# Three cell visits moved to the borders between the feed-forward's products, and the gate products of later chunks moved in front of a mix, into a feed-forward bank

## The chip, the cores and the metric

The kernel runs on one core of a Trainium2 chip. The metric is device time in microseconds (us). TensorE does the matrix products, VectorE and GpSimd the elementwise work, ScalarE the activations, SyncE issues the DMAs (transfers between HBM and on-chip memory). Each engine works through its own queue in order and waits on semaphores of the others. Products land in PSUM, eight banks of 128 partitions by 512 floats; a bank can be written anew once its last reader is through.

## The reference

Two blocks follow each other: an mLSTM cell over 4 batches, 8 heads, 768 steps and head size 40, and a feed-forward block with leaky ReLU, 320 to 2048 to 320, over all 3072 tokens.

```python
for t in range(S):
    m_new = np.maximum(f_gate[:, :, t] + m, i_gate[:, :, t])
    f_stab = np.exp(f_gate[:, :, t] + m - m_new)
    i_stab = np.exp(i_gate[:, :, t] - m_new)
    m = m_new
    C = f_stab[:, :, None, None] * C + i_stab[:, :, None, None] * np.einsum('bhd,bhe->bhde', vt, kt)
    n = f_stab[:, :, None] * n + i_stab[:, :, None] * kt
    h_tilde = np.einsum('bhde,bhe->bhd', C, qt)
    nq = np.einsum('bhd,bhd->bh', n, qt)[:, :, None]
    denom = np.maximum(np.abs(nq), 1.0)
    o = 1.0 / (1.0 + np.exp(-o_gate[:, :, t]))
    y[:, :, t] = o * h_tilde / denom
...
h = x @ w_in
g = np.maximum(0.01 * h, h)
return (g @ w_out).astype(np.float32)
```

## The kernel before

**Chunks and groups.** The 768 steps are cut into six chunks of 128. A *step* `s` of the program is one chunk of one batch, `s = 4c + b`, 24 in all. The recurrence within a chunk is done with matrix products over two halves of 64 steps, and a state is carried from half to half and chunk to chunk. The feed-forward block of chunk `g` (512 tokens, called a group) runs on TensorE while the cells of later chunks are worked out. The cells are cut into pieces and put between the feed-forward's matmuls by hand.

**Feed-forward units.** An ordinary group has 30 units. The *first product* has 8 pairs, each in two units (`pair` in `ff_units`): a pair owns two banks `ph`, its first unit takes 12 matmuls (L909, weights of 64 rows by 128 columns), its second 8, and then two leaky ReLUs on ScalarE (L917) write the activations `acts` and so free the banks. The *second product* (`fast_units`) is a Strassen-like scheme with seven products for each of two token blocks, 14 units of 16 recorded matmuls each (L984, 128 by 128 weights, bank `po`), in the order p1, p2, p6, p7, p4, p5, p3. p1's result is copied by ScalarE (L1003) and `acts` blocks are summed in place by VectorE (L1002 after p1(0) and p1(1), L1007 after p1(1)); p2 is added by VectorE (L1011), which frees its bank; p6, p7 and p4 are copied by ScalarE and added by GpSimd; p5 and p3 are added by VectorE (L1036, L1041). p6 needs the sums of L1007, p7 reads `s3_at` by the weight mix `t3`.

Units are numbered through: group 1 has units 0 to 29 (first product 0 to 15, second 16 to 29), group 2 has 30 to 59 (30 to 45, 46 to 59), group 3 has 60 to 89. Groups 4 and 5 (`three_units`) compute their first product in three parts and have no cells between. The work planned for a unit stands directly behind the unit's matmuls in every queue.

**Cells between the units.** From chunk 2 on, two steps are done at a time. `ready(s)` (READY) transposes keys and queries on VectorE (L537), multiplies queries by decays (L543), and lets GpSimd carry the state on (L630), place the values (L391), scale the keys to `vu` (L510) and mask the decays (L482), whose exponentials ScalarE takes in small portions (L490) in front of later units. A *visit* (VISITS, `u_parts`) issues what remains of the exponentials, and then the score products and state sums on TensorE (`sd`, L652 and L657, 64-row and 64-column weights). VectorE multiplies the scores by the decays (L662, into `qn`) and adds to the state (L634). After the visit stands `feed`, the DMAs of the step four later. A *mix* (MIXES, `u_mix`) multiplies `qn` by state and values on TensorE (`pT`, L745, 128-row and 64-column weights), then VectorE transposes (L752), takes denominators, gates (L756), and GpSimd scales (L759), VectorE transposes back (L763), and the result goes out to `x_dr`, from which `gather_x` reads `xT` for the next group.

**Gate products.** `gates` and `gates_exp` work out a chunk's cumulative gates; `gates_T` (L341) transposes them on TensorE into a tile `tg` (L344, L349, 32-row weights), which VectorE copies out to `gT` and `gL` (L354, L356). `state_next` and the exponentials of the following chunk need these. Units UG say where this is done for chunks 3, 4 and 5.

**Banks.** There are two pools of four PSUM banks: `psf` (tag `mm`) for the feed-forward's `ph` and `po`, `psc` (tag `c`) for the cells' tiles `sd`, `pT` and `tg`. Within a pool a new tile takes a bank whose last tile has been released, and TensorE waits for the engine that reads that tile last.

The plan of the middle stage is this (L1207 on):

```python
VISITS = (5, 14, 27, 35, 46, 58, 67, 76)
MIXES = (7, 17, 29, 37, 51, 60, 69, 77)
READY = ((7, 8), (18, 25), (32, 33), (41, 42), (51, 54), (62, 66), (69, 72))
GATES = ((1, 4), (20, 25), (38, 44))
UG = (18, 37, 62)
PER = NF + 14
```

Of the kernel before, what the change touches and what calls it, by code (L numbers as in the profile page):

```python
# [10 lines left out]
F32 = mybir.dt.float32  # L11
# [11 lines left out]
def kernel(  # L23
# [28 lines left out]
    P = 128  # L52
    BH = B * H
    NB = S // P
# [24 lines left out]
    psf = ctx.enter_context(tc.tile_pool(name="psf", bufs=4, space=PSUM))  # L79
    psc = ctx.enter_context(tc.tile_pool(name="psc", bufs=4, space=PSUM))  # L80
# [257 lines left out]
            nc.tensor.matmul(t[:], lhsT=ident[:], rhs=ident[:], start=True, stop=True)  # L338

    def gates_T(c, bu):  # L340
        tg = psc.tile([P, 5, BH], F32, name="tg", tag="c")  # L341
        kinds = 3 if c == 1 else 2
        for n in range(kinds):
            nc.tensor.transpose(tg[:, n, :], bu[:, n, :], ident[:BH, :BH])  # L344
        gT[c] = wk.tile([P, 3, BH], F32, name="gT")
        if c > 0:
            for u in range(2):
                last = SL * (u + 1) - 1
                nc.tensor.matmul(  # L349
                    tg[:, 3 + u, :], lhsT=bu[:, 2, last : last + 1].to_broadcast([BH, P]), rhs=ident[:BH, :BH],  # L350
                    start=True, stop=True,
                )
            gL[c] = f0[:, ts(c % 2, 2 * BH)].rearrange("p (u n) -> p u n", u=2)
        nc.vector.tensor_copy(gT[c][:, :kinds], tg[:, :kinds, :])  # L354
        if c > 0:
            nc.vector.tensor_copy(gL[c], tg[:, 3:, :])  # L356
# [424 lines left out]
    def open_parts():  # L781

        cells_stack.close()
        kp = ctx.enter_context(tc.tile_pool(name="kp", bufs=1))
        for key in ("raw", "low", "dif"):
            parts["w", key] = [kp.tile([P, WC], F32R, name=f"w_{key}{n}") for n in range(QN)]
        for key in ("low", "dif"):
            parts["x", key] = kp.tile([P, B, KC * P], F32R, name=f"x_{key}")
        parts["tmp"] = [kp.tile([P, KC * P], F32, name=f"tmp{n}") for n in range(2)]
        parts["n"] = 0  # L790
# [255 lines left out]
    def u_gates(c):  # L1046
        gates_T(c, bus.pop(c)[0])
# [78 lines left out]
    def first_chunk():  # L1126

        ffs, narrow = [], {}

        def ff(j, b0, b1):  # L1130
            if not ffs:
                ffs.extend(ff_units(0))
            ffs[0](j, b0, b1)

        def step(n, e=None):
            if (n, e) not in narrow:
                narrow[n, e] = narrow_weights(n, e)
            next(narrow[n, e], None)

        acts_of = {  # L1140
            "ld": load, "lo": load_o, "lw": load_weights, "g": gates, "ge": gates_exp, "warm": warm,
            "ug": lambda c: gates_T(c, bus[c][0] if c == 0 else bus.pop(c)[0]),
            "tr": u_transpose, "tc": transpose_copy, "ab": lambda n: spread_first(bus[0][1], n), "abw": spread_mask,
            "exp": lambda n: run(prep_exp(n)), "vu": prep_vu, "tiles": prepare_tiles, "sc": u_scores, "scm": scores_mix,
            "st": state, "stc": state_copy, "val": u_values, "den": values_den, "o": prep_o, "gate": gate,
            "gp": gate_scale, "nw": step, "ps": prepare_step, "x": u_x, "xc": x_copy, "ff": ff,
            "warmer": warmer, "idle": idle, "fd": feed, "ll": load_late,
        }
        for line in ORDER.split("\n"):
            for what in line.split(";"):  # L1150
                name, *args = what.split() or [None]
                if name:
                    acts_of[name](*map(int, args))
        return ffs[1]

    E = mybir.EngineType
    with tc.manual_schedule(engines={E.PE, E.DVE, E.Activation, E.Pool}):
# [46 lines left out]
                    if s + NL < NS:  # L1204
                        feed(s + NL)

        VISITS = (5, 14, 27, 35, 46, 58, 67, 76)  # L1207
        MIXES = (7, 17, 29, 37, 51, 60, 69, 77)
        READY = ((7, 8), (18, 25), (32, 33), (41, 42), (51, 54), (62, 66), (69, 72))
        GATES = ((1, 4), (20, 25), (38, 44))  # L1210
        UG = (18, 37, 62)
        PER = NF + 14
        SPLIT = (82, 83, 84, 85, 86, 87, 90, 91, 93, 96, 99, 102)
        plan = collections.defaultdict(list)
# [1 line left out]
        def at_unit(unit, fn, *args):  # L1216
            plan[unit].append((fn, args))

        def visit_steps(p):
            return (2 * B + 2 * p, 2 * B + 2 * p + 1) if p < len(VISITS) else ()  # L1220

        def gather():

            while at["past"] and mixed_steps and mixed_steps[0] // B == at["group"] + 1:
                gather_x(mixed_steps.pop(0))
# [22 lines left out]
        mixed_steps = []  # L1248
        for p, unit in enumerate(VISITS):
            c = 2 + p // 2  # L1250
            if p % 2 == 0 and c + 1 < NB:
                at_unit(GATES[p // 2][0], gates, c + 1)
                at_unit(GATES[p // 2][1], gates_exp, c + 1)
            for s in visit_steps(p):
                at_unit(unit, u_parts, s)
            for s in visit_steps(p + 2):
                at_unit(unit, feed, s)
            for s in visit_steps(p):
                at_unit(MIXES[p], mix, s)
            for s in visit_steps(p + 1):  # L1260
                at_unit(MIXES[p], load_late, s, 2)
            if p % 2 == 1 and c + 1 < NB:
                at_unit(UG[p // 2], u_gates, c + 1)
            for n, s in enumerate(visit_steps(p + 1)):
                at_unit(READY[p][n], ready, s)

# [14 lines left out]
        for g in range(1, NB):  # L1281
# [3 lines left out]
            for i in range(len(ffs)):  # L1285
# [8 lines left out]
                gather()  # L1294
                if unit == MIXES[-1]:
                    open_parts()
# [38 lines left out]
```

## Time and profile before

| what | us |
|---|---|
| median of 3 runs | 486.96 |
| lowest and highest | 486.33, 487.30 |
| the profiled execution, its own time | 486.61 |
| its span in the profile | 484.5 |
| TensorE busy | 478.6 |
| VectorE busy | 364.6 |
| ScalarE busy | 196.1 |
| GpSimd busy | 159.4 |

The span is from the first to the last recorded instruction; the 2.1 us between it and the execution's own time lie around it. The granted TensorE clock is full throughout (1.0). Rows of the chain of waits give the start of a piece and its length, both in us, the engine, the tile and the line; `x20` is the number of instructions merged. Rows of a timeline give start, length, engine, line, operation, the tiles written and read with their shapes, and in brackets how long the engine had been idle before and what ended that. PE is TensorE, DVE is VectorE, ACT is ScalarE, POOL is GpSimd, SPq the queue of DMAs that SyncE issues.

### The profile page before, as it was taken

What the parts mean: (1) busy time and instruction counts of PE and PEld (TensorE: products, weight loads), DVE (VectorE), ACT (ScalarE), POOL (GpSimd) and SP (SyncE); (2) the same over time, 40 slices, a digit from 0 to 9 for tenths busy, and PEclk for the clock granted to TensorE, in tenths of its full rate; (3) what the DMA queues carried; (4) which work ended last, traced back from release to release, by engine and by line L of the source; (5) the groups of instructions that cost most, each with busy time, mean ns of one, the idle gap of its engine ahead of it and who ended that gap; (6) DMA issues with size and microseconds to landing.
All of it is one profiled execution on the core that took longest, in us unless ns stands there. A gap on an engine that the chain in (4) does not pass through costs nothing.

```text
span 484.5 us, 12804 instructions
## 1 busy us (share of the span) xinstructions
PE 478.6 (99%) x5113; PEld 371.8 (77%) x5113; DVE 364.6 (75%) x601; ACT 196.1 (40%) x499; POOL 159.4 (33%) x207
## 2 busy tenths in 40 slices
PE   8999999999999999999999999999999999999997
PEld 7998655777645489965569985548998899988996
DVE  4689999889917999777887968689899967335611
ACT  2587864743831331405251121524025642156310
POOL 4128024461601826545451645453210002000020
PEclk9999999999999999999999999999999999999999
DMA  7878778896655677667887867774151030100001
GB/s 144 172 164 195 172 163 169 260 211 146 141 129 111 150 144 212 137 158 194 148 193 171 191 149 177 184 183 123 54 225 40 1 108 1 49 8 0 1 1 54
DMA packets 142698, 63.40 MB, mean 131 GB/s; under 512 B 110832, under 2 KB 130864, under 8 KB 142640
## 3 DMA queue, kind: packets, MB, share of 16 engines
q1 hardware_dynamic: 142256, 62.47, 54.4%
q8 instruction: 40, 0.66, 0.6%
q10 hardware_dynamic: 384, 0.13, 0.1%
q14 instruction: 18, 0.15, 0.1%
HBM read 51.68 MB, written 8.27 MB: 124 GB/s over the span
## 4 chain that ended last, share of the span: by engine, by line
PE 95%; DVE 1%; issue 0%; POOL 0%; POOLq 0%; DVEq 0%
PE po L984 32%; PE ph L909 29%; PE ph L835 8%; PE po L945 7%; PE pe L835 4%; PE pT L745 3%; PE sd L652 3%; PE warm L338 2%; PE pa L675 1%; PE sd L657 1%; PE hN L715 1%; PE tk L566 1%; PE tq L552 1%; PE sc L595 1%; PE tkq L580 0%; PE tg L349 0%
## 5 line engine op out<-in xcount | busy, mean ns | idle before, releaser
L909 PE MATMUL ph<-xT,w_in 64*128 64x512 f32 (+1 forms) x680 | 142.3, 569 | 0.0
L909 PEld LDWEIGHTS ph<-xT,w_in 64*128 64x128 f32 x680 | 64.5, 187 | 66.1 <-issue 63.7
L984 PE MATMUL po<-w_out,acts 128*128 128x160 f32 x640 | 91.0, 301 | 0.0
L984 PEld LDWEIGHTS po<-w_out,acts 128*128 128x128 f32 x640 | 87.5, 190 | 3.4 <-ACT w L490 1.5
L917 ACT ACTIVATE acts<-ph 128x512 f32<-128x512 f32 (+1 forms) x68 | 35.1, 567 | 80.3 <-PE ph L909 80.1
L490 ACT ACTIVATE w<-w,gT 128x64 f32<-128x64 f32 (+1 forms) x192 | 51.8, 348 | 28.1 <-POOL w L482 28.1
L630 POOL TENSOR_TENSOR S<-S,f 40x336 f32<-40x336 f32 x36 | 33.9, 941 | 81.2 <-PE pT L745 47.3
L984 PE MATMUL po<-raw,acts 128*128 128x160 f32 x320 | 45.1, 299 | 0.0
L984 PEld LDWEIGHTS po<-raw,acts 128*128 128x128 f32 x320 | 44.0, 190 | 0.0
L1017 POOL TENSOR_TENSOR y<-y,raw 128x160 f32<-128x160 f32 x10 | 5.5, 556 | 112.2 <-ACT y L1016 112.2
L662 DVE TENSOR_TENSOR qn<-w,sd 64x512 f32<-64x512 f32 x40 | 27.4, 684 | 19.9 <-PE sd L657 11.9
L945 PE MATMUL po<-w_out,acts 128*128 128x320 f32 x128 | 36.6, 437 | 0.0
L482 POOL TENSOR_TENSOR w<-w,i 128x512 f32<-128x512 f32 x20 | 32.4, 1618 | 11.7 <-DMA w<-a_dr 11.7
L857 DVE SCALAR_TENSOR_TENSOR acts<-ph,acts 128x512 f32<-128x512 f32 x32 | 20.6, 685 | 20.6 <-ACT acts L855 20.6
L543 DVE TENSOR_TENSOR qn<-kqT,late 64x512 f32<-64x512 f32 x32 | 33.6, 1049 | 1.0
L945 PEld LDWEIGHTS po<-w_out,acts 128*128 128x128 f32 x128 | 23.6, 190 | 9.1
L759 POOL TENSOR_TENSOR xb<-xb,den 128x320 f32<-128x320 f32 x16 | 11.7, 728 | 48.6 <-DVE xb L756 48.6
L855 ACT ACTIVATE acts<-pe 128x512 f32<-128x512 f32 x32 | 17.4, 595 | 19.0 <-PE pe L835 18.9
L763 DVE STREAM_TRANSPOSE x<-xb 128x512 f32<-128x512 f32 x16 | 17.8, 1109 | 7.8 <-POOL xb L759 7.8
L861 ACT ACTIVATE acts<-acts 128x512 f32<-128x512 f32 x32 | 19.7, 633 | 8.1 <-DVE acts L857 8.1
L984 PE MATMUL po<-raw 128*128 128x160 f32 x160 | 22.7, 300 | 0.0
L652 PEld LDWEIGHTS sd<-kqT 40*64 40x64 f32 x640 | 19.6, 135 | 3.7 <-issue 3.7
(166 smaller groups left out, 786.1 us busy)
## 6 DMA issues: line engine op xcount, KB each, us to landing
w<-a_dr SPq DMA_DIRECT2D x40, 128.0 KB, 3.7
rb<-in_k_dram SPq DMA_DIRECT2D x64, 80.0 KB, 2.8
rb<-in_q_dram SPq DMA_DIRECT2D x64, 80.0 KB, 2.6
rb<-in_o_gate_dram SPq DMA_DIRECT2D x64, 80.0 KB, 2.8
xT<-x_dr SPq DMA_DIRECT2D x32, 160.0 KB, 3.1
late<-a_dr SPq DMA_DIRECT2D x32, 128.0 KB, 3.2
x_dr<-x SPq DMA_DIRECT2D x16, 256.0 KB, 3.0
kn<-in_k_dram SPq DMA_DIRECT2D x24, 160.0 KB, 3.4
```

The costliest lines, as they stand in the source:

```text
L482: nc.gpsimd.tensor_tensor(w, w, cm2.unsqueeze(1).to_broadcast([P, H, SL]), op=ALU.add)
L490: yield nc.scalar.activation(w[:, h, :], w[:, h, :], AF.Exp, bias=gT[c][:, 0, bh : bh + 1], scale=1.0)
L543: nc.vector.tensor_tensor(mixed(s)[rows, 1 - r], d["kqT"][rows, 1].rearrange("p (h t) -> p h t", t=SL), d["ea"][rows], op=ALU.mult,)
L630: nc.gpsimd.tensor_tensor(new, old, g, op=ALU.mult)
L652: nc.tensor.matmul(bank[1 - u][toks, h, :], lhsT=kqT[rows, 0, ts(h, SL)], rhs=kqT[rows, 1, ts(h, SL)], start=True, stop=True,)
L662: nc.vector.tensor_tensor(mixed(s)[toks, u], w[toks], bank[1 - u][toks], op=ALU.mult)
L835: nc.tensor.matmul(ph[r][:], lhsT=parts["w", key][n][part, at : at + P], rhs=xs[key][part, slot, :], start=start and slot == 0, stop=stop ...
L857: nc.vector.scalar_tensor_tensor(fs[r], in0=ph[r][:], scalar=1.0 + EPS, in1=fs[r], op0=ALU.mult, op1=ALU.add,)
L909: nc.tensor.matmul(ph[r][:, cols], lhsT=w_row(r, slot, j), rhs=xT[DP * r : DP * (r + 1), slot, bs, :], start=(slot == 0), stop=(slot == KC ...
L917: nc.scalar.activation(acts[:, f, cols], ph[r][:, cols], AF.Prelu, alpha=0.01)
L945: nc.tensor.matmul(po[n][:], lhsT=acts[:, f, ts(n, P)], rhs=w_out[:, f, :], start=(f == 0), stop=(f == NF - 1),)
L984: nc.tensor.matmul(bank[:], lhsT=left[:, f, :], rhs=right[:, f, :], start=f == 0, stop=f == KH - 1)
```

## The change

Visits 14, 46 and 58 become 15, 45 and 59: the last unit of group 1's first product, the last of group 2's first product and the last of group 2's second. The mix of unit 60 goes to 61. The gate products of chunk 3 go from unit 18 to 17, those of chunk 5 from 62 to 61, so that all three (17, 37, 61) share a unit with a mix, and within the unit they now stand in front of it. Their tile takes a bank of the feed-forward's pool for chunks 3, 4 and 5 (chunks 0 to 2 keep the cells' pool). With the visits the feeds behind them move on SyncE's queue as well: at unit 45 in front of the gathers of `xT`, at unit 59 behind the last output store. As the changed file has one line more in `gates_T`, its later lines are one higher than those of the profile before.

```diff
     def gates_T(c, bu):
-        tg = psc.tile([P, 5, BH], F32, name="tg", tag="c")
+        pool, tag = (psf, "mm") if c > 2 else (psc, "c")
+        tg = pool.tile([P, 5, BH], F32, name="tg", tag=tag)
...
-        VISITS = (5, 14, 27, 35, 46, 58, 67, 76)
-        MIXES = (7, 17, 29, 37, 51, 60, 69, 77)
+        VISITS = (5, 15, 27, 35, 45, 59, 67, 76)
+        MIXES = (7, 17, 29, 37, 51, 61, 69, 77)
...
-        UG = (18, 37, 62)
+        UG = (17, 37, 61)
...
             for s in visit_steps(p + 2):
                 at_unit(unit, feed, s)
+            if p % 2 == 1 and c + 1 < NB:
+                at_unit(UG[p // 2], u_gates, c + 1)
             for s in visit_steps(p):
                 at_unit(MIXES[p], mix, s)
             for s in visit_steps(p + 1):
                 at_unit(MIXES[p], load_late, s, 2)
-            if p % 2 == 1 and c + 1 < NB:
-                at_unit(UG[p // 2], u_gates, c + 1)
```

## The prediction

> **What bounds the kernel now.** I read the page first (busy shares and the chain that ended last), then the chain of waits in order of time around the visits that move, then the timelines of VectorE, ScalarE, GpSimd and SyncE at the same places. Times in chain rows are start and length in us.
>
> ```profile
> span 484.5 us, 12804 instructions
> PE 478.6 (99%) x5113; PEld 371.8 (77%) x5113; DVE 364.6 (75%) x601; ACT 196.1 (40%) x499; POOL 159.4 (33%) x207
> ...
> PE 95%; DVE 1%; issue 0%; POOL 0%; POOLq 0%; DVEq 0%
> ```
>
> TensorE sets the end: 95% of the chain is its own. It waits for nobody here, so only what its stream itself costs can be saved. That cost has a part which isn't arithmetic, the start of each run of matmuls of one tile shape:
>
> ```profile
> 139.62 4.29 PE ph L909 x20
> ...
> 145.93 4.49 PE ph L909 x20
> ```
>
> The first row is twenty feed-forward matmuls cut out of a longer run, the second twenty directly behind a cell visit: 0.20 us more for the same work. The second product shows the same:
>
> ```profile
> 168.09 0.17 PE sd L652
> ...
> 170.10 1.92 PE ph L909 x8
> 172.01 4.54 PE po L984 x32
> 176.56 2.02 PE pT L745 x64
> 178.57 2.37 PE po L984 x16
> 180.94 0.24 PE tg L344 x2
> 181.18 0.45 PE tg L349 x4
> ```
>
> Thirty-two `po` matmuls take 4.54, sixteen take 2.37, so sixteen more cost 2.17 and a start costs 0.20. That it hangs on the tile shape and not on a mere change of tile is seen in chunk 0's second product:
>
> ```profile
> 104.38 2.35 PE po L945 x8
> ...
> 119.41 2.16 PE po L945 x8
> ```
>
> The first eight stand behind the gate product (32-row weights), the second behind full 128-row transposes: 2.35 against 2.16.
>
> **The change, part by part.** No instruction is added or removed on any engine; GpSimd's order is the same line for line. What changes is how often TensorE's stream changes shape. A start is paid by whatever follows the border, so I count the runs that vanish.
>
> Visit at unit 14, mix at 17, gates at 18: now `ph | sd | ph x8 | po x32 | pT | po x16 | tg | po`. After it (visit at 15, gates in front of the mix at 17): `ph | sd | po x32 | tg | pT | po`. One `ph` start and one `po` start go: -0.40.
>
> Visit at 46, now at 45:
>
> ```profile
> 249.60 2.37 PE po L984 x16
> ```
>
> `ph | po x16 | sd | po` becomes `ph | sd | po`: one `po` start, -0.20.
>
> Visit at 58, mix at 60, gates at 62, now 59, 61, 61:
>
> ```profile
> 284.49 2.37 PE po L984 x16
> 286.86 2.78 PE ph L909 x12
> 289.63 2.02 PE pT L745 x64
> 291.65 4.49 PE ph L909 x20
> 296.14 0.24 PE tg L344 x2
> ...
> 296.83 10.50 PE ph L909 x48
> ```
>
> `sd | po x16 | ph x12 | pT | ph x20 | tg | ph` becomes `sd | ph x20 | tg | pT | ph`: one `po` and one `ph` start, -0.40. At unit 37 the gates only change sides with the mix (`pT | tg` to `tg | pT`): no run fewer, 0. Sum of starts: five, -1.0 us.
>
> Unknown in it: `pT` directly behind `tg` is in no row. `pT` takes 2.02 behind `ph` and behind `po`, and `tg` 0.69 behind either or behind `pT`, so I take both as they are. Bounds for the three places: a further start each, +0.6, or one hidden under the other's small weights each, -0.6.
>
> Next, does any wait become late on TensorE? The built program of the changed kernel names for each bank what frees it. The tightest is the second product's seventh unit, p7(0) (`s3_at` by `t3`), whose bank is that of p2(0), freed by VectorE's L1011 (L1012 afterwards). VectorE's queue there:
>
> ```profile
> 145.17 1.39 DVE L662 TENSOR_TENSOR qn<-w,sd 64x512 f32<-64x512 f32 x2 [10.30 <-PE sd L657]
> ...
> 166.13 2.60 DVE L543 TENSOR_TENSOR qn<-kqT,late 64x512 f32<-64x512 f32 x2
> ...
> 170.02 1.38 DVE L662 TENSOR_TENSOR qn<-w,sd 64x512 f32<-64x512 f32 x2
> ...
> 175.97 2.34 DVE L1007 TENSOR_TENSOR acts<-acts 128x1024 f32<-128x1024 f32 x2
> 178.24 0.70 DVE L752 STREAM_TRANSPOSE late<-pT 128x512 f32<-128x512 f32 x1
> ...
> 186.06 0.32 DVE L1011 TENSOR_TENSOR y<-raw,po 128x160 f32<-128x160 f32 x1
> 186.30 0.22 DVE L354 COPY gT<-tg 128x64 f32<-128x64 f32 x1
> ...
> 186.56 1.29 DVE L537 STREAM_TRANSPOSE kqT<-rb 128x512 f32<-128x512 f32 x2
> 187.89 1.55 DVE L543 TENSOR_TENSOR qn<-kqT,late 64x512 f32<-64x512 f32 x2
> 189.48 0.32 DVE L1011 TENSOR_TENSOR y<-raw,po 128x160 f32<-128x160 f32 x1
> ```
>
> A visit takes 170.10 - 168.09 = 2.01, so the one before the `ph` run at 145.93 began at 143.92, and an idle VectorE began its score products 1.25 behind that, at 145.17. The visit at 15 starts at 168.09 + 8 x 0.2145 = 169.81 (0.2145 is 4.29/20), so VectorE begins at 171.06 instead of 170.02, 1.04 later. Its queue is full from there to L1011, and the two gate copies now stand in front of the mix (186.30 to 186.56, 0.26). So L1011 ends at 186.06 + 0.32 + 1.04 + 0.26 = 187.68. TensorE wants that bank here:
>
> ```profile
> 188.18 4.51 PE L984 MATMUL po<-raw 128*128 128x160 f32 x32
> ```
>
> With two starts gone that is 187.78. Margin 0.1 instead of 1.8: I take 0, with 0 to +0.3 for the range. The next bank behind VectorE, p4(0)'s, waits for the second L1011: 189.80 + 1.04 = 190.84, wanted at 187.78 + 4.34 = 192.12, 1.3 to spare.
>
> At unit 45 the thirteen exponentials still open run without p1's copy between them:
>
> ```profile
> 250.60 1.54 ACT L490 ACTIVATE w<-w,gT 128x64 f32<-128x64 f32 x6
> ...
> 258.06 2.34 DVE L1007 TENSOR_TENSOR acts<-acts 128x1024 f32<-128x1024 f32 x2
> ...
> 260.54 4.51 PE L984 MATMUL po<-raw,acts 128*128 128x160 f32 x32
> ```
>
> They end at 250.60 + 13 x 0.257 = 253.94. VectorE then has the second step's products and state (1.8, as 145.17's kind) and both sums L1002 (2.3) ahead of the first L1007 (1.2): about 259.3. p6(0) wants it at 260.34. Hidden, 1.0 to spare. Were the cover gone, each microsecond more is one on TensorE.
>
> At unit 61 the mix comes 2.2 us later against the work behind it, and with it VectorE and GpSimd up to visit 67:
>
> ```profile
> 296.78 0.73 POOL L759 TENSOR_TENSOR xb<-xb,den 128x320 f32<-128x320 f32 x1 [2.42 <-DVE xb L756]
> 299.17 0.76 POOL L630 TENSOR_TENSOR S<-S,f 40x336 f32<-40x336 f32 x1 [1.66 <-DVE f L356]
> ...
> 306.26 0.72 POOL L510 TENSOR_TENSOR vu<-kn,gT 128x320 f32<-128x320 f32 x1
> ```
>
> The mix's last GpSimd product moves from 297.51 to about 299.6, but its successor no longer waits 1.66 for the gate copy, so `vu` of the second step ends at 306.98 + 0.5 = 307.5. The visit starts at 306.83 + 0.1 (the 48-run ends at 307.33, less 0.40), and its second step needs `vu` 1.0 later, 307.9. Margin 0.4: 0, up to +0.2.
>
> SyncE's DMAs: the feeds of the three visits change places with `xT` gathers and two output stores, the same number in all. The feed and `xT` land many units ahead of use, and no compute engine waits for a DMA in this part. Cost 0.
>
> In the feed-forward banks the gate tile takes one of four, so at units 38 and 62 the pair's second bank is the one whose ReLU has only just been issued:
>
> ```profile
> 293.60 1.09 ACT L917 ACTIVATE acts<-ph 128x512 f32<-128x512 f32 x2 [7.03 <-PE ph L909]
> ```
>
> The first of the two frees it 0.55 behind the pair's end, under `tg` and `pT` (0.69 + 2.02 = 2.71). Cost 0; without that cover 0.55 at each place. The rule on the other side is a rival below.
>
> Sum: -1.0 + 0. The profiled execution took 486.61, so 485.6 by its own time; it lies 0.35 below the median of the runs shown, 486.96. The result will be a median, so I name **486.0**.
>
> **The rivals.** (1) *Starts come back.* `tg` beside `pT` costs a start at all three places: -1.0 + 0.6 = -0.4, 486.6. For it: every border of shapes seen so far was charged. Against: the charge shows in the run behind, and `pT` costs 2.02 behind anything.
>
> (2) *The feed-forward rotation is short of a bank.* ReLU isn't hidden at units 38 and 62: +1.1 - 1.0, 487.1, no change. For it: ScalarE may be behind with exponentials. Against: at 293.60 it had idled 7.03 us. The Trainium skill (Perfetto Trace Analysis, Optimizing Tensor Performance) asks that matmul groups rotate through banks so that the eviction of one overlaps the next group; by it a bank lent to the gates would cost here, by the row it doesn't.
>
> (3) *Slower: VectorE's queue at units 17 to 22.* p7(0)'s bank has 0.1 left. The products L543 took 1.55 for two at 187.89 and 2.60 at 166.13 beside GpSimd's work. If the 7.8 us from L752 to L1011 stretched by only 0.3 of itself, L1011 would come 2.4 late, TensorE would stand 2.3, and the net is +1.3, 488.3. It decides from 1.1 late (no gain left); from 2.1 late the kernel is slower by 0.2%. Against: that stretch is the same mix as before with the same GpSimd neighbours, and its order there is unchanged.
>
> **How the numbers follow.** 0.2% (about what a measurement of this kernel can tell from no change) is 0.97 us, right at the forecast gain. The forecast has 0.72, of which I give 0.48 to a gain above 0.97 and 0.24 to one below: each margin worked out above is met, so no stall is the likelier case, but any stall puts it below. Rival 1 has 0.10 and rival 2 0.06, both within 0.2%; rival 3 has 0.12. So faster 0.48, same 0.40, slower 0.12. The range: 486.0 - 0.6 (bound of `tg` with `pT`) is 485.4, and 0.1 for the scatter of the runs makes 485.3; upwards rival 2's 487.1 with 0.1, 487.2. Left out are rival 3 and a little at both ends.
>
> **What would show it.** In the chain of the changed kernel: `sd` followed by `po` x32 of 4.54 without `ph` x8; no `po` x16 of 2.37 on either side of the second and third moved visit; `tg` 0.69 and `pT` 2.02 side by side. Wrong if `pT` there takes 2.2 or `tg` 0.9 (rival 1), if the `ph` run behind the mix at unit 62 begins with a gap until ScalarE's L917 (rival 2), or if the `po` run of units 18 to 29 shows TensorE idle until VectorE's L1012 (rival 3).

## The result, and the profile after

The changed kernel took 485.72 us, the median of 10 runs (485.18 to 486.36), against 486.97 for the kernel before (10 runs): the ratio is 0.9977, with a 95% interval of 0.9968 to 0.9987. That is 1.25 us less, where 486.0 and 1.0 less were forecast. Measured a second time, beside the first experiments, it took 486.11 against 486.82: 0.9988 (0.9979 to 0.9996).

The chain that ended last, of the kernel after, in order of time (start and length in us):

```profile
130.67 13.08 PE ph L910 x60
...
171.65 4.54 PE po L985 x32
176.19 0.24 PE tg L345 x2
176.43 0.45 PE tg L350 x4
176.87 2.02 PE pT L746 x64
178.89 22.04 PE po L985 x160
...
231.77 17.37 PE ph L910 x80
...
251.51 13.24 PE po L985 x96
264.75 2.02 PE pT L746 x64
266.76 17.58 PE po L985 x128
286.36 4.56 PE ph L910 x20
290.92 0.24 PE tg L345 x2
291.15 0.45 PE tg L350 x4
291.60 2.02 PE pT L746 x64
293.62 13.07 PE ph L910 x60
...
363.33 2.52 PE ph L836 x18
```

All five runs are gone: behind the first moved visit stands `po` x32 and no `ph` x8, no `po` x16 of 2.37 stands on either side of the second and third, and `tg` (0.69) and `pT` (2.02) stand side by side at their old lengths.

For comparing traces I take one stretch, from the start of chunk 1's feed-forward (the `ph` x60 above) to the first product of group 4 (L836 above). In the chain of the kernel before its two ends are:

```profile
130.84 13.08 PE ph L909 x60
...
363.97 2.51 PE ph L835 x20
```

The stretch took 233.13 before and 232.66 after: 0.47 less, not 1.0. Ahead of it the two programs are the same but for line numbers, and there the profiled executions scatter: over all the profiles of this study it began between 130.59 and 132.28. That scatter is in every timed run as well; what lies behind the end took 120.3 to 120.5 in every profile. So the times say that the change is faster, by something between 0.2 and 1.6 us, and the stretch says by how much.

Where the other 0.53 went is in three places. The `po` run from 178.89 has 160 matmuls and should take 0.20 + 160 x 0.1359 = 21.94 and took 22.04. (A unit of sixteen costs 2.174, since in the profile before nine units in one run take 19.76 and one takes 2.37; 0.1359 is 2.174/16.) The `ph` run behind the third visit took 4.56 instead of 4.49. And the second visit, which lies between the `ph` run that ends at 249.14 and the `po` run at 251.51, took 2.37 instead of 2.01. The chain of the kernel after within that visit, merged pieces:

```profile
250.07 0.04 PE sd L653 x2
250.10 0.20 PE sd L658
250.30 0.06 issue
250.36 0.24 PE sd L653 x2
```

Pieces of 0.01 to 0.06 are the rule there; 0.20, 0.06 and 0.24 in a row are a stop just where the second step's matmuls begin. VectorE's timeline of the kernel after shows what that step needs:

```profile
237.94 1.10 DVE L764 STREAM_TRANSPOSE x<-xb 128x512 f32<-128x512 f32 x1 [0.36 <-POOL xb L760]
...
241.54 1.39 DVE L301 TENSOR_TENSOR_SCAN m<-fi,il 32x128 f32<-32x128 f32 x1
...
246.31 2.57 DVE L544 TENSOR_TENSOR qn<-kqT,late 64x512 f32<-64x512 f32 x2
248.91 1.30 DVE L538 STREAM_TRANSPOSE kqT<-rb 128x512 f32<-128x512 f32 x2
```

The transposed keys of the second step are ready at 250.2, and TensorE wanted them at 249.14 + 1.0 = 250.1, half a visit behind its start. In the profile before the same instruction was done at 248.71:

```profile
247.41 1.30 DVE L537 STREAM_TRANSPOSE kqT<-rb 128x512 f32<-128x512 f32 x2
```

The bank of p7(0) is the other reading that the prediction hung on. VectorE and TensorE, kernel after, timelines:

```profile
170.92 1.38 DVE L663 TENSOR_TENSOR qn<-w,sd 64x512 f32<-64x512 f32 x2 [1.12 <-PE sd L658]
...
187.24 0.32 DVE L1012 TENSOR_TENSOR y<-raw,po 128x160 f32<-128x160 f32 x1
```

```profile
183.27 4.51 PE L985 MATMUL po<-raw,acts 128*128 128x160 f32 x32
187.62 4.61 PE L985 MATMUL po<-raw 128*128 128x160 f32 x32
```

VectorE releases the bank at 187.56 and the run that needs it starts at 187.62. The run is 4.61 long where its neighbour has 4.51: these are the 0.10. They lie in its first matmul, which took 0.40 where the others took 0.30. In the profile before, the weights of that matmul are loaded at 188.05, 0.13 ahead of the matmul itself (188.18), while the one before it runs. Here the load came only at 187.62, together with its matmul. By these rows the bank is wanted when the weights are loaded, not when the matmul starts.

### The profile page after: what moved, and what is told of

It reads as the page before. It is cut to its first block, busy times and chain, and to the rows that moved or that the text cites. A ratio compares the mean times of both kernels' runs of the same rounds, so it can differ in the third digit from the quotient of the medians.

```text
span 483.7 us, 12813 instructions
## 1 busy us (share of the span) xinstructions
PE 478.0 (99%) x5113; PEld 375.7 (78%) x5113; DVE 364.9 (75%) x601; ACT 195.9 (40%) x499; POOL 160.1 (33%) x207
## 4 chain that ended last, share of the span: by engine, by line
PE 95%; DVE 1%; issue 0%; POOL 0%; POOLq 0%; DVEq 0%
PE po L985 32%; PE ph L910 29%; PE ph L836 8%; PE po L946 7%; PE pe L836 4%; PE pT L746 3%; PE sd L653 3%; PE warm L338 2%; PE pa L676 1%; PE sd L658 1%; PE hN L716 1%; PE tk L567 1%; PE tq L553 1%; PE sc L596 1%; PE tkq L581 0%; PE tg L350 0%
## 5 line engine op out<-in xcount | busy, mean ns | idle before, releaser
L544 DVE TENSOR_TENSOR qn<-kqT,late 64x512 f32<-64x512 f32 x32 | 35.0, 1093 | 1.0
L483 POOL TENSOR_TENSOR w<-w,i 128x512 f32<-128x512 f32 x20 | 31.3, 1567 | 11.6 <-DMA w<-a_dr 11.6
```

Of the source, the lines that this page charges most:

```text
L483: nc.gpsimd.tensor_tensor(w, w, cm2.unsqueeze(1).to_broadcast([P, H, SL]), op=ALU.add)
L544: nc.vector.tensor_tensor(mixed(s)[rows, 1 - r], d["kqT"][rows, 1].rearrange("p (h t) -> p h t", t=SL), d["ea"][rows], op=ALU.mult,)
```

## The experiments

Each row of this table is one kernel: the stretch from its own chain of waits, what it is against before (233.13), and the timed ratio. Each stretch is one profiled execution. Where the interval of a ratio holds 1, the timed runs alone show no change, and the reading rests on the stretch.

| kernel | stretch, us | against before | ratio (95% interval) |
|---|---|---|---|
| changed, first profile | 232.66 | -0.47 | 0.9977 (0.9968 to 0.9987) |
| changed, again | 232.66 | -0.47 | 0.9988 (0.9979 to 0.9996) |
| first border alone | 232.84 | -0.29 | 0.9996 (0.9987 to 1.0005) |
| second border alone | 232.93 | -0.20 | 0.9990 (0.9982 to 0.9999) |
| third border alone | 232.80 | -0.33 | 0.9996 (0.9987 to 1.0005) |
| gates behind the mix at 37 | 232.31 | -0.82 | 0.9971 (0.9956 to 0.9987) |
| keys first | 232.32 | -0.81 | 0.9981 (0.9964 to 0.9998) |
| gates apart at 36 | 232.57 | -0.56 | 0.9976 (0.9959 to 0.9992) |
| gate tile in the cells' bank | 234.44 | +1.31 | 1.0016 (0.9998 to 1.0034) |
| both waits taken away | 232.26 | -0.87 | 0.9978 (0.9969 to 0.9988) |

**The change once more.** No edit.

> The changed kernel once more, unaltered. Theory (five run starts of 0.20 us saved on TensorE, less three small waits of 0.36, 0.10 and 0.07 us seen in the first trace): in the chain of waits the score products of the visit at unit 45 again take 2.37 us instead of 2.01, the second-product run behind the mix of unit 17 again 22.04 instead of 21.94, and the shift of TensorE between the start of chunk 1's feed-forward and the end is again -0.47 us against before; the time is 0.4 to 1.3 us below before. Rival (the waits are chance and differ between executions): the visit at 45 takes 2.01 in this trace, and the shift is -0.8 to -1.0 us.

The stretch was 232.66 again, to the hundredth. The `po` run behind the mix took 22.03 and the `ph` run behind the visit at 59 took 4.56 again. The visit at 45 took 2.37 and had the same stop:

```profile
250.87 0.20 PE sd L658
251.07 0.05 issue
251.12 0.24 PE sd L653 x2
```

So the three waits are not the chance of one execution.

**The first border alone.**

```diff
-        VISITS = (5, 15, 27, 35, 45, 59, 67, 76)
-        MIXES = (7, 17, 29, 37, 51, 61, 69, 77)
+        VISITS = (5, 15, 27, 35, 46, 58, 67, 76)
+        MIXES = (7, 17, 29, 37, 51, 60, 69, 77)
...
-        UG = (17, 37, 61)
+        UG = (17, 37, 62)
...
-        pool, tag = (psf, "mm") if c > 2 else (psc, "c")
+        pool, tag = (psf, "mm") if c in (3,) else (psc, "c")
```

Here and below, a chunk that is not named there keeps its gate products behind the mix; only in the kernel with the gate tile in the cells' bank do they stay in front.

> Only the first border: visit 14 to 15 and chunk 3's gate products to unit 17 in front of the mix, in a feed-forward bank; the rest as before. Theory: two run starts gone (-0.40 us) and the wait for the bank of the fourth product of unit 18 (+0.10): TensorE is 0.30 us earlier at visit 27 than before, nothing changes after it, and the visit at 46 takes 2.01. Rival (moving the gates in front of the mix costs or gains by itself): other than 0.2 to 0.4 us, or a changed visit at 46.

The stretch was 0.29 shorter than before, the `po` run behind the mix took 22.04 again, and the visit at 46 took 2.01: two starts saved, 0.10 lost at p7(0).

**The second border alone.** Only visit 46 goes to 45; mixes and gates stay as before. Against the kernel before:

```diff
-        VISITS = (5, 14, 27, 35, 46, 58, 67, 76)
+        VISITS = (5, 14, 27, 35, 45, 58, 67, 76)
```

> Only the second border: visit 46 to 45; the gate products stay behind the mix in the cells' bank. Theory A (the wait in visit 45 comes from the visit's being 2.4 us earlier): the visit at 45 takes 2.1 to 2.4 us, net 0 to +0.2. Theory B (it comes from the gates standing in front of the mix at 37, which lets GpSimd start earlier and collide with VectorE's scans): the visit takes 2.01 and the net is -0.20 us.

The stretch was 0.20 shorter, and the visit at 45 took 2.01, between these two rows of the chain:

```profile
231.99 17.37 PE ph L910 x80
...
251.37 13.24 PE po L985 x96
```

231.99 + 17.37 = 249.36, and 2.01 on is 251.37. The earlier visit alone doesn't wait: theory A fell.

**The third border alone.** Visit 58 to 59, mix 60 to 61, gates 62 to 61 in front of it in a feed-forward bank; the rest as before.

> Only the third border: visit 58 to 59, mix 60 to 61, chunk 5's gate products to 61 in front of the mix, in a feed-forward bank. Theory: two run starts gone, -0.40 us less 0.07 in the first-product run behind the visit; the visit at 67 takes 2.01 (its last input, the scaled keys, is ready 0.4 us before). Rival (GpSimd or VectorE late at visit 67): that visit takes 2.2 or more and the net is above -0.2.

The stretch was 0.33 shorter. Visit 67 doesn't wait. The 0.07 behind the visit at 59 is there again (4.56). The three alone sum to -0.82; together they give -0.47. The 0.35 between is the stop in the visit at 45. It is not there with the early visit alone; the next kernel asks whether it needs the gates of unit 37 in front of the mix as well.

**Gates of unit 37 behind the mix.** The changed kernel, but chunk 4's gates behind the mix and in the cells' bank.

```diff
-        pool, tag = (psf, "mm") if c > 2 else (psc, "c")
+        pool, tag = (psf, "mm") if c in (3, 5) else (psc, "c")
```

> The changed kernel with chunk 4's gate products alone (unit 37) put back behind the mix and into the cells' bank. Theory (the gates in front let GpSimd start early and collide with VectorE, which makes the keys late for the visit at 45): that visit takes 2.01 again and TensorE, from the start of chunk 1's feed-forward to the first product of group 4, takes 232.30 us, 0.83 less than before and 0.36 less than the changed kernel. Rival (the wait is due to the other moves together): the visit still takes 2.2 to 2.4.

The stretch was 0.82 shorter than before, and the visit took 2.01: the stop needs the early visit and the gates in front of the mix together. VectorE's timeline of this kernel, to be held against the rows after:

```profile
237.37 1.14 DVE L764 STREAM_TRANSPOSE x<-xb 128x512 f32<-128x512 f32 x1 [0.36 <-POOL xb L760]
...
241.29 0.65 DVE L301 TENSOR_TENSOR_SCAN m<-fi,il 32x128 f32<-32x128 f32 x1
...
245.27 2.14 DVE L544 TENSOR_TENSOR qn<-kqT,late 64x512 f32<-64x512 f32 x2
247.44 1.31 DVE L538 STREAM_TRANSPOSE kqT<-rb 128x512 f32<-128x512 f32 x2
```

From the mix's last transpose to the end of the second keys it is 11.4 us here; the same work, without the two gate copies in it, took 12.3 in the changed kernel (237.94 to 250.2). L301 took 0.65 here and 1.39 there, L544 2.14 and 2.57. Measured from the start of the stretch, the changed kernel has these keys ready 1.7 later than the kernel before: 0.9 is the slower work, and 0.7 is that the mix's last transpose itself starts later (107.27 behind the start of the stretch, against 106.53). By these numbers the keys would have been in time if only one of the two had come. GpSimd's timelines, first this kernel, then the changed one:

```profile
239.04 1.61 POOL L631 TENSOR_TENSOR S<-S,f 40x336 f32<-40x336 f32 x1 [1.70 <-DVE f L357]
240.70 0.97 POOL L392 COPY S<-w 64x320 f32<-64x320 f32 x2
```

```profile
237.98 0.76 POOL L631 TENSOR_TENSOR S<-S,f 40x336 f32<-40x336 f32 x1
238.79 1.84 POOL L392 COPY S<-w 64x320 f32<-64x320 f32 x2
```

With the gates copied out early GpSimd no longer waits 1.70 for them, starts its state and value work at once, and stands beside other instructions of VectorE. That this is what slowed VectorE is argued from the two timelines; the gates-apart kernel below shows that an early start of GpSimd doesn't always do it.

**Keys first.** The changed kernel with VectorE's work for the visit at 45 in another order: keys of both steps are transposed before the queries of either are multiplied (`decay_q` is the last loop of `prep_kq`).

```diff
-            prep_kq(s)
-            if s + NR < NS:
+            two = s // 2 == B + 4
+            prep_kq(s, two)
+            if two:
+                load_late(s + NR, 0)
+                load_late(s + NR, 1)
+                for n in (s - 1, s) if s % 2 else ():
+                    decay_q(n)
+                    spread_q(n + NR)
+            elif s + NR < NS:
```

> The changed kernel; for the two steps of the visit at 45 VectorE transposes the keys of both before it multiplies the queries of either (same work, other order). Theory (the visit at 45 waits for the transposed keys of its second step, which stand behind 2.6 us of query products): the visit takes 2.01, the stretch 232.30 us. Rival (it waits for GpSimd's scaled keys or the state instead): still 2.2 to 2.4.

The stretch was 0.81 shorter than before, and the visit took 2.01. VectorE's timeline there has the keys done at 247.2:

```profile
244.75 2.47 DVE L538 STREAM_TRANSPOSE kqT<-rb 128x512 f32<-128x512 f32 x4
247.15 3.76 DVE L550 TENSOR_TENSOR qn<-kqT,late 64x512 f32<-64x512 f32 x4
```

The gates still stand in front at 37 here, and GpSimd's scaled keys of the second step are ready no earlier than in the changed kernel (2.09 ahead of the visit's start here, 2.49 there), nor is the carried state (3.87 and 5.64). So it was the transposed keys, and neither GpSimd's scaled keys nor the state, that TensorE waited for. The order is not the only difference: VectorE reached these keys 6.6 behind the mix's last transpose here and 7.0 in the changed kernel, by the same instructions. But with 3 us to spare, these 0.4 don't decide.

**Gates apart.** The changed kernel with one run of a tile shape more.

```diff
-        UG = (17, 37, 61)
+        UG = (17, 36, 61)
```

> The changed kernel with chunk 4's gate products one unit earlier (36), between two feed-forward runs of their own, so that TensorE's stream has one run more. Theory (each run of one tile shape pays a start of 0.20 us): the stretch is 0.20 us longer than the changed kernel's 232.66, or less if the visit at 45 waits less. Rival (the 0.20 belongs to something else than the start of a run): no change.

```profile
225.20 2.78 PE ph L910 x12
227.97 0.24 PE tg L345 x2
228.21 0.45 PE tg L350 x4
228.66 1.92 PE ph L910 x8
230.57 2.02 PE pT L746 x64
```

The twenty `ph` matmuls take 2.78 + 1.92 = 4.70 in two runs, 4.49 in one: the start is 0.21. The stretch was 0.09 shorter than the changed kernel's, not longer, since here the visit at 45 took 2.01 (-0.36), and the run behind the visit at 59 lost 0.06 more: 0.21 - 0.36 + 0.06 = -0.09. The rival, that the 0.20 belongs to something other than the start of a run, fell by the two runs' 0.21; the stretch by itself could not tell.

Why the visit didn't wait is seen in VectorE's and GpSimd's timelines there:

```profile
238.76 1.11 DVE L764 STREAM_TRANSPOSE x<-xb 128x512 f32<-128x512 f32 x1 [0.36 <-POOL xb L760]
...
248.76 1.31 DVE L538 STREAM_TRANSPOSE kqT<-rb 128x512 f32<-128x512 f32 x2
```

```profile
238.80 0.76 POOL L631 TENSOR_TENSOR S<-S,f 40x336 f32<-40x336 f32 x1
```

GpSimd starts its state work 0.04 behind the start of VectorE's transpose, as in the changed kernel (237.98 and 237.94), and both engines have the same instructions in the same order from there to the keys. Yet VectorE took 11.3 here and 12.3 there: L301 0.97 and 1.39, the first two L544 2.02 and 2.57, and GpSimd's first two copies 2.15 and 1.84. So an early GpSimd alone does not make the keys late. What tips the two engines into the slow overlap is not shown.

**The gate tile in the cells' bank.** Everything moved as in the change, the tile's pool alone undone.

```diff
-        pool, tag = (psf, "mm") if c > 2 else (psc, "c")
+        pool, tag = psc, "c"
```

> The changed kernel with the gate tile left in the cells' four banks, everything else moved as in the change. Theory (two of these banks are held from the visit to the mix's state sums, so the second mix tile must wait until VectorE has copied the gates out): at unit 17, where VectorE is 2.9 us behind, the mix takes 1.5 to 2 us longer than 2.02, and the stretch is about 234.2 us, 1.0 longer than before; at 37 and 61 no wait. Rival (any bank does): 232.66 as in the changed kernel.

The stretch was 1.31 longer than before. TensorE's timeline there shows the second mix tile waiting for the copy of the gates:

```profile
178.41 1.15 PE L746 MATMUL pT<-qn,S 128*64 128x64 f32 x32
181.24 1.15 PE L746 MATMUL pT<-qn,S 128*64 128x64 f32 x32 [1.68 <-DVE f L357]
```

The mix takes 3.91 there instead of 2.02. At 37 and 61 it takes 2.02. The bank is what makes the place in front of the mix usable at unit 17.

**Both waits taken away.** Gates of chunk 4 behind the mix, and mix and gates of unit 17 at 18.

```diff
-        MIXES = (7, 17, 29, 37, 51, 61, 69, 77)
+        MIXES = (7, 18, 29, 37, 51, 61, 69, 77)
...
-        UG = (17, 37, 61)
+        UG = (18, 37, 61)
...
-        pool, tag = (psf, "mm") if c > 2 else (psc, "c")
+        pool, tag = (psf, "mm") if c in (3, 5) else (psc, "c")
```

> The changed kernel with both waits taken away: chunk 4's gate products behind the mix of unit 37 in the cells' bank, and chunk 3's gate products and the mix of unit 17 both one unit later, at 18, so that VectorE adds the second product's third unit ahead of the mix and its bank is free in time. Theory (five starts of 0.20 saved and only the 0.07 behind the visit at 59 lost): the run behind that mix costs 2.17 per unit and 0.20 for its start without the 0.10, and the stretch from the start of chunk 1's feed-forward to the first product of group 4 is 232.2 us, 0.93 less than before; the time is 0.5 to 1.5 us below before, 0.45 below the changed kernel. Rival (VectorE's later mix makes another bank late): the run of units 19 to 29 keeps a gap, the stretch stays at 232.3 or more.

```profile
172.66 6.72 PE po L985 x48
...
182.08 19.76 PE po L985 x144
...
286.91 4.63 PE ph L910 x20
```

Both `po` runs now cost their start and 2.174 a unit, nothing more: VectorE's L1012 for p2(0) ended at 180.47 there, ahead of the mix's work. The run behind the visit at 59 lost 0.14 instead of 0.07, so the stretch is 232.26, 0.40 less than the changed kernel's. The times (485.88, ratio 0.9978) can't tell the two apart.

## Why the prediction came out as it did

- *What bounds the kernel.* Right. TensorE has 95% of the chain after as before, and only its stream could be shortened.
- *Five run starts of 0.20, -1.0.* Right in number and size. Alone, the borders gave -0.29, -0.20 and -0.33; with the losses that each trace shows (0.10, 0, 0.07) these are -0.39, -0.20 and -0.40. One run more in the gates-apart kernel cost 0.21. What the prediction said a start hangs on, the tile shape, is less sure. The row just ahead of the `po` x8 of 2.16 is `119.30 0.11 PE xt L879`, a transpose with weights of 128 rows by 64 columns. That is the size of `pT`'s weights, and behind `pT` a `po` run does pay 0.20. So the size of the weights doesn't decide alone. `pT`'s matmuls start in pairs 0.01 apart, the transposes one by one 0.11 apart; whether that is the difference was not tried. The Trainium skill (TensorEngine Tiling, Key Properties) states that a change of tiling mode, and not just of tile, drains TensorE; the charged borders would fit that, but no row names the mode.
- *`pT` directly behind `tg`.* 2.02 and 0.69, as taken; rival 1 fell.
- *p7(0)'s bank.* VectorE was reckoned to free it at 187.68 for a run at 187.78. In the trace after, whose stretch began 0.17 earlier, it was 187.56 for 187.62. The 0.10 lies in the bounds that were given (0 to 0.3); the value taken, 0, was too low. The step held the release against the start of the matmul, and the weights are loaded 0.13 ahead of it: against 187.65, a release at 187.68 is late already. Rival 3's mechanism was there at a tenth of a microsecond; its price was not reached.
- *Unit 45, "Hidden, 1.0 to spare".* This step failed. It checked the exponentials and the sums behind the visit, and not the transposed keys of the visit's second step. By the rows of before these were ready in time (at 248.71, where TensorE would want them at 249.60 - 0.40 + 1.0 = 250.2), but neither their start nor the durations ahead of them were to be carried over: the sentence that GpSimd's order is unchanged priced its shift in time at nothing. With the gates ahead of the mix, the mix's VectorE work came 0.7 later and the work from there to the keys took 0.9 longer beside GpSimd, and together these made the keys late. It cost 0.36, a third of the gain. That the keys were waited for, and that the stop goes when the gates stand behind the mix, is shown by runs; that GpSimd slowed VectorE is argued.
- *Visit 67.* No wait, as forecast: it took 306.69 to 308.70, 2.01.
- *The bank for the gates.* The ReLU behind the mix was hidden at both places (the `ph` runs there took 17.37 for 80 and 13.07 for 60, a start and 0.2145 a matmul), rival 2 fell, and the rule of the Trainium skill that was weighed there had no price here. Without the bank the change would have been slower: +1.31 in the stretch, though the timed ratio of that kernel holds 1 in its interval.
- *The time.* The two measured gains, 1.25 and 0.71, lie on either side of the forecast 1.0, but the stretch says 0.47. That the medians came so near the forecast is luck: half of the five starts was lost again, and the prediction had given twice the chance to a gain above 0.97 (0.48) as to one below (0.24). The first measurement's interval (0.63 to 1.56) leaves that out by a little, and the second's holds it; I take the stretch for the effect of the change, and the rest for the scatter, most of it ahead of the stretch. That was only argued, not tried.

Left open are the 0.07 to 0.14 in the `ph` run behind the visit at 59. They lie in the run's first two matmuls, which together take 0.77 in the kernel after, 0.83 in the gates-apart kernel and in the one with both waits taken away, and 0.70 behind the visit at 67. It is the first run of group 3, and why its second matmul starts late no experiment took apart. Open too is what tips VectorE and GpSimd into the slow overlap.

## What to carry to other kernels

Where one engine is busy throughout, count the runs that pay a start: here each cost 0.20 us, and moving interleaved work to a border that exists anyway saves one. Read from the rows which borders are charged, since the size of the weights alone doesn't tell. Then check every input of what was moved, not the last one alone, hold a bank's release against the load of the weights, and don't carry VectorE's or GpSimd's durations over when the two engines' work slides against each other. An effect smaller than the scatter of the timed runs can still be read from a stretch of the trace whose ends don't move for other reasons; the one kernel that was profiled twice gave the same stretch to the hundredth.

## What was not expected of the hardware

The same VectorE work took 11.4 or 12.3 us with GpSimd's work beside it placed otherwise: a scan of 32 by 128 elements 0.65 or 1.39, two query products 2.14 or 2.57, and GpSimd's own two copies 0.97 or 1.84. In the gates-apart kernel it took 11.3, though both engines had the same instructions in the same order as in the changed kernel and began 0.04 apart in both.

The Trainium skill (SBUF — State Buffer, SBUF: two separate sides) states that VectorE's instructions with two inputs in SBUF, against GpSimd's that read SBUF, take a shared pair of ports as an exclusive lock, the later one waiting the whole instruction out. Durations that differ in such pairs are what it would lead one to expect. No run here had the lock alone to itself, and GpSimd's spans in a profile are rough, so that it is the cause is not shown.

TensorE's stretch of 233 us repeated to 0.01 us from one execution to the next (232.66 twice), while the start of that stretch moved by up to 1.7 us between profiles.
